# Attention and two MLP layers: row maxima by pair of heads, one turn per pair, and four weight blocks decoded in the first layer

## The chip, the cores and the metric

One core of a Trainium2 chip runs the whole program. The metric is device time in microseconds of one execution; the median of several runs counts. The kernel before was run three times: 1042.83, 1044.88 and 1046.16 us, median 1044.88 us.

## What is computed

The reference, cut to what matters (32 heads of 576 rows and 64 columns, 2304 tokens, widths 512, 2048 and 1024; tau is 0.02):

```python
scores = scale * np.matmul(q, k.transpose(0, 1, 3, 2))
thresh = np.max(scores, axis=-1, keepdims=True) - tau
scores = np.where(scores >= thresh, scores, -1000000000.0)
scores = scores - np.max(scores, axis=-1, keepdims=True)
attn = np.exp(scores)
attn = attn / (np.sum(attn, axis=-1, keepdims=True) + 1e-09)
x = heads_side_by_side(np.matmul(attn, v))

h = x @ w_in                                     # first layer
g = np.where(h >= 1, h, np.where(h <= -1, 0.0, (h + 1) ** 2 / 4))
x = g @ w_out

h = x @ w_in2                                    # second layer
e = np.exp(h - np.max(h, axis=-1, keepdims=True))
solu = h * e / (np.sum(e, axis=-1, keepdims=True) + 1e-09)
ln = (solu - mean(solu)) / np.sqrt(var(solu) + 1e-06) * g_ln
out = ln @ w_out2
```

The four weight matrices arrive as 64-bit floats, which the kernel turns into 32-bit ones itself, block by block ("decoding").

## The kernel before, in words

Engines are named as in the profile: PE multiplies matrices, DVE and ACT work on tiles, POOL too (but not on PSUM, the accumulator memory), and SP issues most transfers. Every fp32 factor is split in a high and a low part, so that three matmuls stand for one product. The order of the instructions on each engine is the order in which the program is written; nothing is reordered afterwards.

**Attention** goes through 16 pairs of heads, nine *units* to a pair, 144 units in all. A unit has 128 key rows of one head; the fifth unit of a pair has the last 64 rows of the first head and the first 64 of the second. For unit u, `attention_unit(u)` runs through a string of letters, each a piece of work:

- S: `scores`, 128 query rows against all 576 keys of a head, four matmuls, and x: `row_max`, the maximum of each row of that tile on DVE. These belong to a later pair, since the maxima of all query rows are wanted before a pair's exponentials. The numbers `S_UNITS` say how many units ahead each of a pair's ten tiles is made.
- A and P, shortly after a head's last tile: `row_shift` (two small operations on ACT, three on POOL) makes the shift from the maxima, `shift_turn` transposes it on PE (tile `tm`), and `shift_store` copies it (tile `mt`) and sends it by a transfer into rows of `q_m`, whence the next product has the shift added.
- E: `shifted`, the shifted scores of the unit, keys by queries (tile `zt`, four matmuls, eight in the shared unit), and `expo` on ACT; M: `mask` on DVE sets to zero what lies below the threshold; p: `p_split` makes high part (`phi`, ACT) and low part (`plo`, POOL) of the unit before; v and V: `values`, the product with V of three units before, six matmuls (`av`).
- P also: `transpose_kq`, five transposes (tile `tr`) for one head of a later pair; F: `split_kq`, high part on ACT and low part `lo` on DVE; T: `stack_k` and `stack_q`, four transfers that put those parts where `scores` and `shifted` read them, and `load_kq` (eight transfers) and `load_v` (three). L: `store_head`.
- J: a step of the decode jobs. A block of 128 x 512 weights is one load, one ACT operation, five DVE operations (L487, L490, L493, L497, L500, on the path `words_to_f32`) and one POOL addition; blocks for use at once then are split on ACT and POOL (`to_sbuf`), others go back to DRAM (`to_dram`). `DECODE` says in which units of a pair which step may run, and `JOB_EVERY` how many units lie between two blocks.

The tiles `sc`, `zt`, `tm` and `tr` share a ring of three PSUM buffers (`ps_r`). A fourth tile must wait until the first has been read: `sc` by `row_max`, `zt` by `mask`, `tm` by the copy to `mt`, `tr` by the split to `lo`.

```python
    ps_r = scores_ps.enter_context(tc.tile_pool(name="ps_r", bufs=3, space=PSUM))
    ...
    jobs = Jobs(parts(("in1", 0), ("out1", 0)) + ahead_out2(0, 1, 2, 3), JOB_EVERY, 2)
```

Twelve blocks are decoded beside the attention: eight of the first layer, and four of the second layer's output weights, ahead of their use.

**First layer.** The 2048 hidden columns are taken in four groups; in each, five chunks of tokens (three of 512, two of 384) meet four blocks of 128 columns. A step n is `moe1_in` (12 matmuls, `h`), `moe1_act` (`cl`, `gh`, `gl` on DVE, ACT and POOL), and `moe1_out` of two steps before (12 matmuls, `y`). Beside a group the blocks of the next are decoded, one begun every three job steps, and what is left at the group's last step is done there at once (`jobs.finish()`). The second layer follows; the change touches nothing in it.

Of the kernel before, what the change touches and what calls it, by code (L numbers as in the profile page):

```python
# [21 lines left out]
def kernel(  # L22
# [45 lines left out]
    ORDER = (  # L68
        "FESvSxvMxxpVPLTASJ",
        "vFEvSSTSxxMxxxpLVPAJ",  # L70
        "EvvvSSSMxxxVLFPATpJ",
        "FESvSSxxMxxpVLPATJ",
        "FESSSMJvxxxpVLPAT",
        "FEvvSSSMxxxpVLPATJ",
        "FvJEvSSSMxxxpVLPAT",
        "FEvvvSSSMxxxVLPvATpJ",
        "FSEvPSSTMxxxpVLAJ",
    )
    STACK = (1, 3)
    V_AT = -5  # L80
    FAST = 2
    V_POOL = 10
    LO_UNITS = ()
    NORM = (13, 5)
    LO_DVE = ()
    T_FIRST = (-17, -17)
    T_SECOND = (-13, -2)
# [4 lines left out]
    DECODE = ('', '', 's', 'asb', '', 's', '', 'as', 'asb')  # L92
# [50 lines left out]
    NBUF = (3, 2)  # L143

    def key_off(h):
        return 64 * (h % 2)

# [29 lines left out]
    def setup_fill(first):  # L177

        for i in range(max(NBUF)):
            for j in range(2):  # L180
# [7 lines left out]
                nc.gpsimd.memset(f32(q_st[j][i][:, S:SP]), 0.0)  # L188
                nc.gpsimd.memset(f32(q_m[j][i][0:D, S:SP]), 0.0)
# [75 lines left out]
    def split_kq(h):  # L265
# [3 lines left out]
        hi = q_st[j][i][:, 0:S]  # L269
# [6 lines left out]
    def stack_k(h):  # L276
        j, i = buf(h)
        kh = f32(q_st[j][i][0:D, 0:S])
        o = slice(key_off(h), key_off(h) + S)
        if h < FAST:  # L280
            nc.scalar.copy(k_on[j][i][0:D, o], kh)
            nc.scalar.copy(q_m[j][i][0:D, 0:S], f32(q_st[j][i][D:P, 0:S]))
# [15 lines left out]
    def scores(h, n):  # L298
        j, i = buf(h)
        o = key_off(h)  # L300
        ps = ps_r.tile([P, 2, 512], F32, tag="r", name="sc")
        for st, kk in ((q_st, k_st), (q_m, k_on)):
            r = slice(0, P if st is q_st else R1)
            for c in range(2):
                nc.tensor.matmul(  # L305
                    ps[:, c, 0:HS],
                    lhsT=st[j][i][r, n * P : n * P + P],
                    rhs=kk[j][i][r, o + c * HS : o + (c + 1) * HS],
                    start=(st is q_st),
                    stop=(st is q_m),  # L310
                )
        sc_ps[h, n] = ps

    def row_max(h, n):
        if n == 0:
            mcol[h] = att_p.tile([P, NTI], F32, tag="mcol", name="mcol", bufs=2)
        mc = mcol[h]
        nc.vector.tensor_reduce(  # L318
            mc[:, n : n + 1], sc_ps.pop((h, n))[:, :, 0:HS], axis=AXES.XY, op=ALU.max, negate=True
        )  # L320

    def row_shift(h):
        mc = mcol.pop(h)


        sh = att_p.tile([P, 2, NTI], F32, tag="sh", name="sh", bufs=2)
        mr = att_p.tile([P, 2, NTI], F32R, tag="mr", name="mr", bufs=2)
        nc.scalar.activation(out=sh[:, 0, :], in_=mc, func=ACTF.Abs, scale=DELTA)
        nc.scalar.activation(out=sh[:, 1, :], in_=sh[:, 0, :], func=ACTF.Relu, bias=ntau[:, 0:1], scale=1.0)
        nc.gpsimd.tensor_tensor(sh[:, 0, :], sh[:, 1, :], mc, op=ALU.add)  # L330
        nc.gpsimd.tensor_copy(mr[:, 0, :], sh[:, 0, :])
        nc.gpsimd.tensor_tensor(mr[:, 1, :], sh[:, 0, :], f32(mr[:, 0, :]), op=ALU.subtract)
        mr_t[h] = mr
# [767 lines left out]
```

## Time and profile before

| what | value |
|---|---|
| three runs, us | 1042.83, 1044.88, 1046.16 |
| the profiled execution's own time, us | 1043.3 |
| its span, first to last instruction, us | 1041.5 |
| PE busy, share of the span | 93% |
| DVE, ACT, POOL busy | 70%, 51%, 57% |
| attention, first to last matmul of the stage | about 6 to 407 us |
| first layer | about 408 to 832 us |
| mean granted clock of PE | 0.993 of full speed |

The time is the execution as the device counts it; the span leaves out 1.8 us around the instructions. A busy share is an average over stages, so the argument goes by stretches. In the rows, L305 is a line of the kernel before, `sc<-k_both,q_st` a matmul that writes tile `sc`, and x4 means four instructions. A time in square brackets behind a row is idle time of that engine before it, and what ended it.

### The profile page before, as it was taken

How to read it: one execution, taken by the hardware profiler on the slowest of the kernel's cores; microseconds unless marked ns; L12 is line 12 of the kernel's file. 1: busy time of each engine (PE TensorE's matmuls, PEld its weight loads, DVE VectorE, ACT ScalarE, POOL GpSimd, SP SyncE). 2: the span in 40 equal slices, each digit the busy share in tenths (PEclk: the TensorE clock that was granted, in tenths of full speed). 3: DMA queues.
4: the chain of work that ended last, by engine and by line, in shares of the span. 5: the costliest groups of instructions: out<-in, count | busy, mean ns of one | idle time of the engine just before them, and what ended most of it. 6: DMA issues, size and time to landing. Idle time of an engine off the chain costs nothing.

```text
span 1041.5 us, 15175 instructions
## 1 busy us (share of the span) xinstructions
PE 969.5 (93%) x5232; PEld 841.7 (81%) x5232; DVE 732.1 (70%) x1133; ACT 535.3 (51%) x1006; POOL 598.0 (57%) x569
## 2 busy tenths in 40 slices
PE   4899899889979998999999999999999999999998
PEld 3788888788878897767887888788888988888886
DVE  3788888868877775588747875787567556666662
ACT  2666666756756666645443443444344534344433
POOL 6577778967786776657524552555256823344332
PEclk9999999989999999999999999999999999999999
DMA  6555556555755520321121112111211104444443
GB/s 155 136 136 135 124 136 160 136 122 131 184 145 126 132 70 24 91 84 59 33 71 61 42 41 81 51 51 41 91 41 51 56 7 132 108 121 127 122 131 91
DMA packets 89885, 99.89 MB, mean 96 GB/s; under 512 B 50032, under 2 KB 62640, under 8 KB 89808
## 3 DMA queue, kind: packets, MB, share of 16 engines
q1 hardware_dynamic: 89424, 98.76, 36.5%
q8 instruction: 41, 0.67, 0.3%
q14 instruction: 36, 0.29, 0.1%
q10 hardware_dynamic: 384, 0.16, 0.1%
HBM read 55.13 MB, written 15.88 MB: 68 GB/s over the span
## 4 chain that ended last, share of the span: by engine, by line
PE 54%; issue 13%; DVE 12%; POOL 10%; ACT 6%; DMA 3%; SPq 2%; ACTq 0%; POOLq 0%; DVEq 0%
PE y L779 10%; PE h L742 10%; PE o L932 10%; PE h L821 9%; PE av L426 6%; PE zt L378 5%; PE sc L305 3%; DVE e L394 3%; POOL gl L763 3%; POOL dec_a L504 2%; POOL plo L403 2%; POOL wg L533 2%; ACT e L389 2%; DVE mcol L318 2%; DMA q_st<-lo 1%
## 5 line engine op out<-in xcount | busy, mean ns | idle before, releaser
L403 POOL TENSOR_TENSOR plo<-e,phi 128x576 fp32r<-128x576 f32 x144 | 206.2, 1438 | 80.7 <-ACT phi L402 79.5
L763 POOL TENSOR_TENSOR gl<-cl,gh 128x512 fp32r<-128x512 f32 (+1 forms) x80 | 96.9, 1211 | 189.4 <-ACT gh L762 156.0
L779 PE MATMUL y<-gh,wg 128*128 128x512 f32 (+1 forms) x640 | 187.6, 374 | 4.1 <-ACT gh L762 4.1
L742 PE MATMUL h<-xh,wg 128*128 128x512 f32 (+1 forms) x640 | 185.8, 371 | 2.0 <-DVE e L394 2.0
L394 DVE SCALAR_TENSOR_TENSOR e<-zt,ntau,e 128x576 f32<-128x576 f32 x144 | 116.6, 810 | 64.9 <-ACT e L389 64.7
L758 ACT ACTIVATE h<-h,mone 128x512 f32<-128x512 f32 (+1 forms) x80 | 49.5, 619 | 198.8 <-DVE cl L757 198.6
L389 ACT ACTIVATE e<-zt 128x576 f32<-128x576 f32 x144 | 93.7, 651 | 96.6 <-PE zt L378 81.1
L779 PEld LDWEIGHTS y<-gh,wg 128*128 128x128 f32 x640 | 117.9, 188 | 24.1 <-ACT gh L762 7.8
L742 PEld LDWEIGHTS h<-xh,wg 128*128 128x128 f32 x640 | 119.0, 189 | 19.2 <-DVE e L394 2.3
L779 PE MATMUL y<-gl,wg 128*128 128x512 f32 (+1 forms) x320 | 122.0, 381 | 10.2 <-POOL gl L763 10.2
L318 DVE TENSOR_REDUCE mcol<-sc 128x1 f32<-128x576 f32 x160 | 116.7, 747 | 10.4 <-PE sc L305 10.4
L757 DVE TENSOR_SCALAR cl<-h 128x512 f32<-128x512 f32 (+1 forms) x80 | 50.8, 635 | 102.0 <-PE h L742 69.0
L742 PE MATMUL h<-xl,wg 128*128 128x512 f32 (+1 forms) x320 | 118.8, 371 | 0.0
L932 PE MATMUL o<-wg,ln 128*128 128x512 f32 x432 | 103.2, 395 | 0.0
L821 PE MATMUL h<-wg,y 128*128 128x512 f32 x432 | 101.2, 390 | 0.0
L402 ACT CAST phi<-e 128x576 fp32r<-128x576 f32 x144 | 96.3, 669 | 2.1 <-DVE e L394 1.9
L932 PEld LDWEIGHTS o<-wg,ln 128*128 128x128 f32 x432 | 81.0, 188 | 19.2
L821 PEld LDWEIGHTS h<-wg,y 128*128 128x128 f32 x432 | 81.0, 188 | 17.0
L896 POOL TENSOR_TENSOR ln<-land,ln 128x1024 fp32r<-128x1024 f32 x16 | 38.5, 2408 | 92.2 <-ACT ln L895 86.4
L378 PE MATMUL zt<-q_st,k_both 128*128 128x288 f32 x320 | 76.9, 322 | 10.4 <-ACT mt L345 5.2
L305 PE MATMUL sc<-k_both,q_st 128*128 128x288 f32 x320 | 73.4, 312 | 13.1 <-DMA q_st<-lo 8.7
L779 PEld LDWEIGHTS y<-gl,wg 128*128 128x128 f32 x320 | 60.1, 188 | 27.3 <-POOL gl L763 19.1
(109 smaller groups left out, 1940.4 us busy)
## 6 DMA issues: line engine op xcount, KB each, us to landing
raw<-in_moe_w_in_dram SPq DMA_DIRECT2D x24, 512.0 KB
raw<-in_moe_w_out_dram SPq DMA_DIRECT2D x24, 512.0 KB
k_both<-q_st SPq DMA_DIRECT2D x30, 288.0 KB
sq<-so SPq DMA_DIRECT2D x64, 128.0 KB
land<-sq SPq DMA_DIRECT2D x16, 512.0 KB
k_both<-lo SPq DMA_DIRECT2D x32, 144.0 KB
q_st<-lo SPq DMA_DIRECT2D x32, 144.0 KB
x<-xs SPq DMA_DIRECT2D x32, 144.0 KB
```

The lines of the kernel that those rows point to most:

```text
L305: nc.tensor.matmul(ps[:, c, 0:HS], lhsT=st[j][i][r, n * P : n * P + P], rhs=kk[j][i][r, o + c * HS : o + (c + 1) * HS], start=(st is q_st) ...
L318: nc.vector.tensor_reduce(mc[:, n : n + 1], sc_ps.pop((h, n))[:, :, 0:HS], axis=AXES.XY, op=ALU.max, negate=True)
L378: nc.tensor.matmul(ps[:, c, 0:HS], lhsT=st, rhs=mv[:, c * HS : (c + 1) * HS], start=(m == 0), stop=(m == len(todo) - 1),)
L389: nc.scalar.activation(out=e, in_=st_ps[u][:, :, 0:HS], func=ACTF.Exp)
L394: nc.vector.scalar_tensor_tensor(out=e, in0=st_ps.pop(u)[:, :, 0:HS], scalar=ntau[:, 0:1], in1=e, op0=ALU.is_ge, op1=ALU.mult)
L402: nc.scalar.copy(hi, e)
L403: (nc.vector if u - NU in LO_DVE or u < NU - UNITS and u % UNITS in LO_UNITS else nc.gpsimd).tensor_tensor(lo, e, f32(hi), op=ALU.subtract)
L742: nc.tensor.matmul(ps, lhsT=a[:, kk, f], rhs=m[:, kk, :], start=(n == 0 and kk == 0), stop=(n == 2 and kk == KD - 1),)
L763: nc.gpsimd.tensor_tensor(gl, cl, f32(gh), op=ALU.subtract)
L779: nc.tensor.matmul(y_ps[c][d], lhsT=a[:, jj, ds_], rhs=m, start=(jj == 0 and n == 0), stop=(jj == JG - 1 and n == 2),)
L821: nc.tensor.matmul(ps[g], lhsT=a[:, kk, :], rhs=wg_t["in2", g][s][:, kk, :], start=(n < 2), stop=(n >= 6 * KD - 2),)
L932: nc.tensor.matmul(ps, lhsT=a[:, f, :], rhs=wg_t["out2", f // 4][m][:, f % 4, :], start=(n == 0), stop=(n == len(terms) - 1))
```

## The change

Row maxima are made by pair. A pair's 1152 query rows now stand in nine tiles of 128, where each head had five for itself, the fifth half empty: the last 64 query rows of the first head and the first 64 of the second share tile 4, into which eight matmuls accumulate. To that end the queries of the second head lie 64 columns further on (`on(h)`), with zeros in the pad, as the keys did already. One `row_max` is left out per pair, and the shared column of maxima is copied on POOL. From the second pair on there is one `row_shift` and one turn for both heads; the store is still two transfers.

All units have the same string of letters, with one tile of scores at its start. Tiles are made 14 to 6 units ahead (10 to 2 before), transposes of keys and queries 22 and 16 units ahead (16 and 10). To hold more heads at a time the second head has three buffers instead of two; `e` has 3 instead of 4 buffers, `phi` and `plo` 4 instead of 5, `xs` and `mt` 1 instead of 2.

Only eight blocks are decoded beside the attention, one begun every 14 units; the four blocks of the second layer's output weights go to the first layer's groups, one more each in the first two and two more in the third.

```diff
-    T_A, T_B = -16, -10
-    S_UNITS = (-10, -9, -7, -7, -6, -5, -4, -3, -3, -2)
+    T_A, T_B = -22, -16
+    S_FIRST = -14
...
-    JOB_EVERY = 9
-    ORDER = (
-        "FESvSxvMxxpVPLTASJ",
...
-    )
+    JOB_EVERY = 14
+    ORDER = "SxFEvMvpVLPATJ"
...
-    V_AT = -5
+    V_AT = -2
-    T_SECOND = (-13, -2)
+    T_SECOND = (-13, -7)
-    DECODE = ('', '', 's', 'asb', '', 's', '', 'as', 'asb')
+    DECODE = ('asb', 's', 'asb', 'a', 'sb', 'asb', 'a', 's', 'asb')
-    NBUF = (3, 2)
+    NBUF = (3, 3)
...
-    def scores(h, n):
+    S_ORDER = (0, 1, 2, 3, 5, 4, 6, 7, 8)
+    def scores(p, n):
         ps = ps_r.tile([P, 2, 512], F32, tag="r", name="sc")
+        todo = []
+        for h in ([2 * p] if n <= 4 else []) + ([2 * p + 1] if n >= 4 else []):
+            j, i = buf(h)
+            at_ = slice((n - 4 * j) * P, (n - 4 * j) * P + P)
+            for st, kk, r in ((q_st, k_st, P), (q_m, k_on, R1)):
+                todo.append((st[j][i][0:r, at_], kk[j][i][0:r, on(h)]))
...
-    def row_max(h, n):
+    def row_max(p, n):
...
+        m = n + (n > 4)
         nc.vector.tensor_reduce(
...
+        if n == 4:
+            nc.gpsimd.tensor_copy(mc[:, 5:6], mc[:, 4:5])
...
-        for j in range(2):
-            t = UNITS * p + S_UNITS[NTI * j + NTI - 1]
-            at(act_, t + 1, row_shift, 2 * p + j)
...
+        for js, last in ((slice(0, 1), 4), (slice(1, 2), 8)) if p == 0 else ((slice(0, 2), 8),):
+            t = UNITS * p + S_FIRST + S_ORDER.index(last)
+            at(act_, t + 1, row_shift, p, js)
+            at(pe_, t + TURN_AT, shift_turn, p, js)
+            at(act_, t + TURN_AT, shift_store, p, js)
...
-    jobs = Jobs(parts(("in1", 0), ("out1", 0)) + ahead_out2(0, 1, 2, 3), JOB_EVERY, 2)
+    jobs = Jobs(parts(("in1", 0), ("out1", 0)), JOB_EVERY, 2)
...
-        parts(("in1", 1), ("out1", 1)) + ahead_out2(4, 5),
-        parts(("in1", 2), ("out1", 2)) + ahead_out2(6, 7),
-        parts(("in1", 3), ("out1", 3)) + ahead_in2(*IN2_AHEAD),
+        parts(("in1", 1), ("out1", 1)) + ahead_out2(0, 1, 2),
+        parts(("in1", 2), ("out1", 2)) + ahead_out2(3, 4, 5),
+        parts(("in1", 3), ("out1", 3)) + ahead_out2(6, 7) + ahead_in2(*IN2_AHEAD),
```

The order of the instructions at three places, before and after. The numbers behind `k_both`, `q_st` and `q_m` tell buffers of different heads apart.

PE at a turn, in the middle of the attention. Before:

```order
L305 MATMUL sc<-k_both_102,q_st_107 128x288 x2
L305 MATMUL sc<-k_both_102,q_m_112 128x288 x2
L426 MATMUL av<-plo,v_hi_117 128x288 x2
L339 MATMUL tm<-ident,mr 10x128
L378 MATMUL zt<-q_st_108,k_both_103 128x288 x2
L378 MATMUL zt<-q_m_113,k_both_103 128x288 x2
```

After:

```order
L382 MATMUL zt<-q_m_114,k_both_102 128x288 x2
L430 MATMUL av<-phi,v_hi_119 128x288 x2
L430 MATMUL av<-phi,v_lo_121 64x288 x2
L430 MATMUL av<-plo,v_hi_119 128x288 x2
L341 MATMUL tm<-ident,mr 20x128
L301 MATMUL sc<-k_both_101,q_st_107 128x288 x2
L301 MATMUL sc<-k_both_101,q_m_113 128x288 x2
L382 MATMUL zt<-q_st_108,k_both_102 128x288 x2
```

The next `zt` stood right behind the turn; now the turn stands at a unit's end, and a tile of scores comes between it and the next `zt`.

DVE at the very start (`lo` rows are the splits of heads 0, 1, 2, 3 and so on). Before:

```order
L271 SCALAR_TENSOR_TENSOR lo<-tr,scale_120,q_st_104 128x576
L271 SCALAR_TENSOR_TENSOR lo<-tr,scale_120,q_st_107 128x576
L271 SCALAR_TENSOR_TENSOR lo<-tr,scale_120,q_st_105 128x576
L318 TENSOR_REDUCE mcol<-sc 128x1 x10
L271 SCALAR_TENSOR_TENSOR lo<-tr,scale_120,q_st_108 128x576
L318 TENSOR_REDUCE mcol<-sc 128x1 x2
L394 SCALAR_TENSOR_TENSOR e<-zt,ntau,e 128x576 x3
```

After:

```order
L262 SCALAR_TENSOR_TENSOR lo<-tr,scale_123,q_st_105 128x576
L262 SCALAR_TENSOR_TENSOR lo<-tr,scale_123,q_st_108 128x576
L315 TENSOR_REDUCE mcol<-sc 128x1 x3
L262 SCALAR_TENSOR_TENSOR lo<-tr,scale_123,q_st_106 128x576
L315 TENSOR_REDUCE mcol<-sc 128x1 x6
L262 SCALAR_TENSOR_TENSOR lo<-tr,scale_123,q_st_109 128x576
L315 TENSOR_REDUCE mcol<-sc 128x1 x3
L262 SCALAR_TENSOR_TENSOR lo<-tr,scale_123,q_st_107 128x576
L315 TENSOR_REDUCE mcol<-sc 128x1 x3
L398 SCALAR_TENSOR_TENSOR e<-zt,ntau,e 128x576
```

The split of head 2 stood ahead of all row maxima and now stands behind three; 15 maxima instead of 12 and one more split stand ahead of the first mask.

DVE at the last step of the first layer's second group. Before:

```order
L757 TENSOR_SCALAR cl<-h_7033 128x384
L761 TENSOR_TENSOR cl<-cl,h_6989 128x384
L497 TENSOR_SCALAR raw<-dec_a 128x512
L500 SCALAR_TENSOR_TENSOR raw<-raw 128x512
L757 TENSOR_SCALAR cl<-h_7075 128x512
L761 TENSOR_TENSOR cl<-cl,h_7033 128x384
```

After:

```order
L766 TENSOR_TENSOR cl<-cl,h_6769 128x384
L501 TENSOR_SCALAR raw<-dec_a 128x512
L504 SCALAR_TENSOR_TENSOR raw<-raw 128x512
L491 TENSOR_SCALAR dec_a<-dec_a 128x512
L494 TENSOR_SCALAR dec_a<-dec_a 128x512
L497 SCALAR_TENSOR_TENSOR dec_a<-raw,dec_a 128x512
L501 TENSOR_SCALAR raw<-dec_a 128x512
L504 SCALAR_TENSOR_TENSOR raw<-raw 128x512
L762 TENSOR_SCALAR cl<-h_6866 128x512
L766 TENSOR_TENSOR cl<-cl,h_6813 128x384
```

All five DVE operations of the added block stand behind the group's last step and ahead of the next step's `cl`. It is so at the end of the first group too, and at the end of the third with two blocks, ten operations.

## Rows read from the trace of the kernel before

**Rows 1.** Windows of one pair each, with decoding and without: busy us (count) by engine.

```profile
57.90:82.00 24.10, 21.90 (x154) 20.08 (x153) 20.87 (x27) 16.31 (x31) 18.62 (x18) 1.00 0.57 133
343.30:365.60 22.30, 21.07 (x153) 19.88 (x152) 16.50 (x23) 15.20 (x29) 15.84 (x17) 1.00 0.50 115
```

**Rows 2.** Waits of PE, 28 to 407 us: us in total, times, longest.

```profile
PE tr L262 <- DVE e L394: 8.6, 14, 1.0
PE tm L339 <- DVE e L394: 6.3, 12, 0.8
PE zt L378 <- ACT mt L345: 5.2, 15, 0.3
PE sc L305 <- DMA q_st<-lo: 5.1, 3, 4.1
PE zt L378 <- DVE lo L271: 4.1, 8, 0.6
```

**Rows 3.** Chain of waits, 0 to 460 us: start, us, what.

```profile
15.47 2.73 DMA q_st<-lo
...
343.26 1.07 PE sc L305 x8
```

**Rows 4.** Timeline of PE: start, us, line, operation.

```profile
13.35 1.38 PE L262 MATMUL tr<-ident,nat 128*128 128x128 f32 x5 [3.90 <-DMA nat<-in_k_dram]
...
28.51 0.42 PE L378 MATMUL zt<-q_st,k_both 128*128 128x288 f32 x2
...
192.59 0.80 PE L262 MATMUL tr<-ident,nat 128*128 128x128 f32 x5
...
197.88 0.27 PE L339 MATMUL tm<-ident,mr 128*10 128x128 f32 x1
...
209.87 0.82 PE L305 MATMUL sc<-k_both,q_st 128*128 128x288 f32 x2 [4.13 <-DMA q_st<-lo]
...
386.04 0.54 PE L378 MATMUL zt<-q_st,k_both 128*128 128x288 f32 x2 [0.34 <-ACT mt L345]
...
402.61 0.42 PE L378 MATMUL zt<-q_st,k_both 128*128 128x288 f32 x2
```

**Rows 5.** Window after PE's longest wait: PE, PEld, DVE, ACT, POOL busy, clock, DMA.

```profile
209.90:214.90 5.00, 5.00 (x21) 4.93 (x22) 1.31 (x2) 1.24 (x3) 1.20 (x4) 0.50 0.76 165
```

**Rows 6.** Timelines of DVE and SP at the start of the program.

```profile
18.32 0.82 DVE L271 SCALAR_TENSOR_TENSOR lo<-tr,scale,q_st 128x576 fp32r<-128x576 f32 x1 [7.24 <-DMA q_st<-lo]
...
21.59 0.76 DVE L318 TENSOR_REDUCE mcol<-sc 128x1 f32<-128x576 f32 x1 [0.20 <-PE sc L305]
...
32.51 0.46 SPq L293 DMA_DIRECT2D q_st<-lo  x1
```

**Rows 7.** Timeline of DVE in a pair with decoding.

```profile
180.06 0.81 DVE L271 SCALAR_TENSOR_TENSOR lo<-tr,scale,q_st 128x576 fp32r<-128x576 f32 x1
180.78 0.74 DVE L318 TENSOR_REDUCE mcol<-sc 128x1 f32<-128x576 f32 x1
181.45 0.80 DVE L394 SCALAR_TENSOR_TENSOR e<-zt,ntau,e 128x576 f32<-128x576 f32 x1
182.18 0.95 DVE L500 SCALAR_TENSOR_TENSOR raw<-raw 128x512 f32<-128x512 uint32 x1
```

**Rows 8.** Groups of DVE instructions, 57.9 to 106.1 us: busy us, mean ns.

```profile
L490 DVE TENSOR_SCALAR dec_a<-dec_a 128x512 uint32<-128x512 uint32 x2 | 3.3, 1631 | 0.0
```

**Rows 9.** First layer, around group ends: timelines of DVE and PE.

```profile
615.52 0.67 DVE L487 TENSOR_SCALAR dec_a<-dec_a 128x512 f32<-128x512 f32 x1
...
618.84 0.69 DVE L500 SCALAR_TENSOR_TENSOR raw<-raw 128x512 f32<-128x512 uint32 x1
...
731.87 0.69 DVE L500 SCALAR_TENSOR_TENSOR raw<-raw 128x512 f32<-128x512 uint32 x1
733.67 0.69 DVE L757 TENSOR_SCALAR cl<-h 128x512 f32<-128x512 f32 x1 [1.11 <-POOL gl L763]
...
738.33 0.52 PE L779 MATMUL y<-gh,wg 128*128 128x384 f32 x2
```

More of the change, by code (lines that the diff above doesn't have):

```diff
@@ L306, in scores @@
                     ps[:, c, 0:HS],
[L307 to L310, printed above, removed]
-                )
-        sc_ps[h, n] = ps
-    def row_max(h, n):
-        if n == 0:
-            mcol[h] = att_p.tile([P, NTI], F32, tag="mcol", name="mcol", bufs=2)
-        mc = mcol[h]
+                    lhsT=st,
+                    rhs=mv[:, c * HS : (c + 1) * HS],
@@ L318, in row_max @@
+                    start=(m == 0),
+                    stop=(m == len(todo) - 1),
+                )
+        sc_ps[p, n] = ps
+    def row_max(p, n):
+        if p not in mcol:
+            mcol[p] = att_p.tile([P, 2, NTI], F32, tag="mcol", name="mcol", bufs=2)
+        mc = mcol[p].rearrange("p j n -> p (j n)")
+        m = n + (n > 4)
         nc.vector.tensor_reduce(
-            mc[:, n : n + 1], sc_ps.pop((h, n))[:, :, 0:HS], axis=AXES.XY, op=ALU.max, negate=True
+            mc[:, m : m + 1], sc_ps.pop((p, n))[:, :, 0:HS], axis=AXES.XY, op=ALU.max, negate=True
@@ L320, in row_max @@
         )
[L322 to L333, printed above, removed]
@@ new lines, with row_shift @@
+    mr_t = {}
+    def row_shift(p, js):
+        mc = mcol[p][:, js, :]
+        sh = att_p.tile([P, 2, 2, NTI], F32, tag="sh", name="sh", bufs=2)
+        mr = att_p.tile([P, 2, 2, NTI], F32R, tag="mr", name="mr", bufs=2)
+        s0, s1, m0, m1 = sh[:, 0, js], sh[:, 1, js], mr[:, js, 0, :], mr[:, js, 1, :]
+        nc.scalar.activation(out=s0, in_=mc, func=ACTF.Abs, scale=DELTA)
+        nc.scalar.activation(out=s1, in_=s0, func=ACTF.Relu, bias=ntau[:, 0:1], scale=1.0)
+        nc.gpsimd.tensor_tensor(s0, s1, mc, op=ALU.add)
+        nc.gpsimd.tensor_copy(m0, s0)
+        nc.gpsimd.tensor_tensor(m1, s0, f32(m0), op=ALU.subtract)
+        mr_t[p, js.start] = mr[:, js]
@@ new lines, in shift_turn, with shift_store @@
+    def shift_turn(p, js):
+        ps = ps_r.tile([P, 1024], F32, tag="r", name="tm")
+        mr = f32(mr_t.pop((p, js.start))).rearrange("p j l n -> p (j l n)")
+        nc.tensor.transpose(ps[0 : mr.shape[1], 0:P], mr, ident)
+        mr_t[p, js.start] = ps[0 : mr.shape[1], 0:P]
+    def shift_store(p, js):
+        mt = att_p.tile([4 * NTI, P], F32R, tag="mt", name="mt", bufs=1)
+        ps = mr_t.pop((p, js.start))
+        nc.scalar.copy(mt[0 : ps.shape[0]], ps)
+        for n, h in enumerate(range(2 * p + js.start, 2 * p + js.stop)):
+            j, i = buf(h)
+            nc.scalar.dma_start(f32(q_m[j][i][R1:R3, :]), f32(mt[2 * NTI * n : 2 * NTI * n + 2 * NTI, :]))
@@ L387, in expo @@
     def expo(u):
-        e = att_p.tile([P, 2, HS], F32, tag="e", name="e", bufs=4)
+        e = att_p.tile([P, 2, HS], F32, tag="e", name="e", bufs=3)
         nc.scalar.activation(out=e, in_=st_ps[u][:, :, 0:HS], func=ACTF.Exp)
@@ L399, in p_split @@
         e = e_t.pop(u)
-        hi = att_p.tile([P, 2, HS], F32R, tag="phi", name="phi", bufs=5)
-        lo = att_p.tile([P, 2, HS], F32R, tag="plo", name="plo", bufs=5)
+        hi = att_p.tile([P, 2, HS], F32R, tag="phi", name="phi", bufs=4)
+        lo = att_p.tile([P, 2, HS], F32R, tag="plo", name="plo", bufs=4)
         nc.scalar.copy(hi, e)
-        (nc.vector if u - NU in LO_DVE or u < NU - UNITS and u % UNITS in LO_UNITS else nc.gpsimd).tensor_tensor(lo, e, f32(hi), op=ALU.subtract)
+        nc.gpsimd.tensor_tensor(lo, e, f32(hi), op=ALU.subtract)
         ph_t[u] = (hi, lo)
@@ L434, in store_head @@
         if h < NH - 2:
-            xs = att_p.tile([P, 2, HS], F32, tag="xs", name="xs", bufs=2)
+            xs = att_p.tile([P, 2, HS], F32, tag="xs", name="xs", bufs=1)
         else:
@@ L691, in attention_unit @@
         mx = iter(s_at.get(u, ()))
-        for what in ORDER[u % UNITS]:
+        for what in ORDER:
             if what == "E" and 0 <= u < NU:
```

52 lines of the change are left out of this document (15 added, 37 removed).

## The prediction, made before the changed kernel ran

> **What bounds the kernel now.** I read the page by engine first: PE is busy for 93% of the span, so only what lets PE work without gaps, or takes work from it, can pay. The change lies in the attention and in the first layer, so next come windows of one pair of heads. A pair with a decoded block lasts 24.1 us, one without 22.3 us; PE issues some 153 matmuls in both, and DVE is busy for 20.87 and 16.50 us of them [rows 1]. So a block costs 1.8 us of the attention, and DVE does not set the pace alone: PE waits between bursts. The table of PE's waits says for what. Three of the five are waits for a ring buffer (`tr` and `tm` for the mask of an earlier `zt`, `zt` for the copy `mt`), 20.1 us in all; `zt` waits 4.1 us for `lo`, and three late transfers cost 5.1 us [rows 2]. The chain and the timeline give PE's floor: eight matmuls of 288 columns in a row take 1.07 us, five transposes at most 0.80, a turn at most 0.27 [rows 3, 4]. A pair has 140 such matmuls, two sets of transposes and, after the change, one turn: 140 x 1.07 / 8 + 1.60 + 0.27 = 20.6 us, or 2.29 us a unit. Both kinds of pair lie above that, by 1.7 and 3.5 us. That is what there is to win here.
>
> The sum is made against the profiled execution, 1043.3 us (span 1041.5 and 1.8 around it); it is 1.6 us below the median of 1044.88.
>
> **The units that hold scores.** Before, the last tile of scores is made in unit 133, and from the first `zt` (28.51) to that unit's (386.04) are 357.5 us, 2.69 a unit. After the change the last tile is in unit 129, so 130 units hold scores.
> - Floor: 130 x 2.29 = 297.5 us. The matmuls of the tile left out are not saved, since the shared tile takes eight; a turn less per pair is in the floor already.
> - Eight blocks remain, at the 1.8 us that a block costs now [rows 1]: 14.4 us. Bounds: nothing, if DVE's room hides them, and 4.4 us each, the whole difference in DVE's busy time. I take the measured price, though the neighbours change: the maximum left out takes off 0.74 us of DVE per pair, while the changed order puts most blocks' five steps into five units in a row.
> - Ring waits: the buffer that `tm` or `tr` takes over was that of the unit before, whose mask is long done; behind `tm` comes a tile of scores, so `zt` meets `mt` late; the wait for `lo` passes to the second tile of scores behind `tr`. A DVE on time needs 0.67 us for the maximum and 0.72 for the split (start to start, [rows 7]); PE comes for that buffer 2.29 - 0.53 = 1.76 us after the scores. That is just in time, so I leave 0.3 us a pair, 4.3 us for 14.4 pairs; bounds are 0 and the 1.7 us of today's pair without a block, 24 us.
>
> Sum: 316 us for 130 units, 2.43 each.
>
> **The start.** The split of head 2 began at 18.32 [rows 6]. Now it stands behind three row maxima. The third begins at 21.59 [rows 6], later by head 2's transposes, which now lie between tiles of scores (1.38 us, [rows 4]), and takes 0.76: the split begins at 23.7, 5.4 us later. On SP behind it stand the stacking of head 2, eleven loads and the stacking of head 3, the same transfers as before, loads of keys and queries now ahead of those of values; all in order, so the last transfer of head 3 goes from 32.51 [rows 6] to 37.8. It lands 2.73 later [rows 3], at 40.6. Before, no early `zt` hung on it; now two tiles of pair 1 that read head 3 (12 matmuls, 1.6 us) stand ahead of the first `zt`. So that comes at 42.1 instead of 28.51. PE is nearly idle for some microseconds before. After its longest wait of today, 4.13 us, it ran the next 5 us at a granted clock of 0.50, which is 1.2 GHz [rows 4, 5], and lost 2.5 us; I add the same. Bounds for both: 6 and 18 us.
>
> **The tail.** Without scores a unit takes (402.61 - 386.04) / 10 = 1.66 us [rows 4]. From the `zt` of unit 130 to that of 143 are 13 x 1.66 = 21.5 us, where it was ten units. The change moves nothing in these units but the size of three buffers.
>
> The last `zt`: 42.1 + 2.5 + 316.2 + 21.5 = 382.3, against 402.61 [rows 4]: **20.3 us earlier**.
>
> **Smaller buffers, DMAs, other queues.** `e`, `phi` and `plo` lose a buffer each; the unit's values run three units behind, so four `plo` still do. SP loses the four blocks' loads and stores, about 8 issues; ACT issues as many stores of `mt` as before, two at a time once a pair. Heads are stacked three to five units ahead of their first tile (two to three before), which covers the late transfers of [rows 2]. POOL gets one tiny copy per pair. I count all this at nothing; what hides it is POOL's idle 5.5 us in a pair [rows 1], and one queue late by a unit would cost about 2.4 us each time.
>
> **The first layer.** A block on DVE takes 618.84 + 0.69 - 615.52 = 4.0 us [rows 9]. By the order the added ones stand behind a group's last step, ahead of the next `cl`. At the third end DVE was done with decoding at 731.87 + 0.69 = 732.6 [rows 9]. With two more blocks `cl` starts at 740.6 instead of 733.67; it takes 0.69, and the addition and the two parts that follow, as three steps of its kind, about 2 us more: 743.3. PE wants that at 738.33 and waits 5 us. With one block `cl` starts at 736.6 and PE waits 0 to 1: 1 us each at the first two ends. Sum **7 us**; bounds 0 (all covered by PE's four `h` buffers) and 16 (four blocks in full).
>
> The decode step L490 takes 1.63 us in the attention [rows 8], where POOL is busy for 77% of a pair [rows 1]. The Trainium skill, "SBUF — State Buffer", section "SBUF: two separate sides", says that DVE and GpSimd (POOL) share a pair of ports under an exclusive lock, and that whoever comes second is fully blocked until the other's instruction ends. By that rule a block would be cheaper at a group's end, where POOL waits for `gh`, and the 7 us would be nearer 5; the row of 4.0 us is from such a stretch already, so my sum keeps it.
>
> **Sum:** 1043.3 - 20.3 + 7 = **1030.0 us**.
>
> **The rivals.**
> 1. *Decoding is hidden.* One maximum less and fewer blocks leave DVE room, so the eight blocks cost PE nothing. For it: DVE is at 87% in today's worst pairs [rows 1] and gets 0.74 us less. Against: five steps in successive units. Time: 1030 - 14.4 = 1016.
> 2. *Slower: a decode step delays the next unit's maximum and split in full.* The place is DVE's queue: a step of up to 1.63 us [rows 8] follows the mask, and behind it stand the maximum and the split on whose buffers PE's next tiles wait, with no unit of respite between two steps. If a block's 4.4 us reach PE whole, the price is 8 x 2.6 = 21 us more: 1051. It decides from 1.8 + 13.3 / 8 = 3.5 us a block. Against: the ring now gives the maximum a whole unit.
> 3. *The change does not do what it says.* Ring waits only change places, and a pair without a block stays at 22.3 us: 14.4 x 1.4 = 20 us more, 1050. For it: the ring still has three buffers for the same operations, and with smaller `e` and `plo` POOL may come late. Against: the 20.1 us of [rows 2] hang on an order that is gone.
>
> **How the numbers follow.** My forecast has a chance of 0.55, with a range of its own from 1018 to 1041 by its bounds (the start 7 us shorter, the first layer 5 us either way, ring waits from 0 to 0.9 us a pair). Rival 1 has 0.20, rival 2 has 0.12, rival 3 has 0.13. A measurement of this kernel tells about 0.3%, 3.1 us, from no change; so faster means below 1041.7 and slower above 1048. Forecast and rival 1 lie below but for a little of the forecast: 0.72. Rivals 2 and 3 in part strength end near no change: 0.12; in full they are slower: 0.16. The range of 8 in 10 reaches to rival 1's better half and to the milder halves of 2 and 3: 1012 to 1048.
>
> **What would show it.** First `zt` near 42 us and the last near 382; a pair near 20.9 us without and 22.7 with a block; the waits of `tr` and `tm` for masks gone from PE's list, and `zt` no longer waiting for `mt`; a granted clock of half for some microseconds after 40 us; at the end of the first layer's third group a wait of about 5 us of `y` for `gh`. The prediction is wrong if a pair without a block stays above 22 us, if a block costs over 3.5 us, or if a new wait (`e` for POOL, `xs` for its store) stands high in the lists of ACT or PE.

## The result, and the profile after

The changed kernel is slower by 1.2%: 1057.26 us, median of four runs (1056.14 to 1058.10), against 1043.86 for the kernel before in the same comparison; ratio 1.0122, 95% interval 1.0104 to 1.0139. The forecast was 1030.0, its range 1012 to 1048. The profiled execution took 1056.5 us (span 1054.7). Against the forecast's own terms:

| term | before | forecast | after |
|---|---|---|---|
| first `zt`, us | 28.51 | 42.1 | 43.24 |
| first to last `zt` | 374.1 | 340.2 | 356.5 |
| last `zt` | 402.61 | 382.3 | 399.72 |
| first layer, first `h` to the second layer's first `h` | 423.6 | 430.6 | 439.0 |
| profiled execution | 1043.3 | 1030.0 | 1056.5 |

So the start came as forecast. The units between missed by 16 us, and the first layer by 8. PE's waits in the attention, 28 to 407 us, after the change (us in total, times, longest):

```profile
PE zt L382 <- DVE mcol L315: 8.4, 10, 1.1
PE sc L301 <- DVE mcol L315: 8.3, 14, 0.8
PE av L430 <- ACT xs L442: 7.5, 10, 1.5
PE sc L301 <- DMA q_st<-lo: 4.8, 1, 4.8
PE sc L301 <- DVE lo L262: 2.2, 6, 0.4
```

The waits of [rows 2] for masks and for `mt` are gone but for 0.2 us, as the prediction said. In their place stand 16.7 us for row maxima (`mcol`), and 7.5 us of the values `av` for the copy `xs`. ACT's list for the same stretch puts 12.6 us of `e` down to `plo` (11 times), which was the other new wait that the prediction named as a sign against it. That line must not be taken at its word: eight of the eleven, 11.5 us together, stand right behind two stores of `mt` that ACT issues itself, as at this turn:

```profile
82.55 0.25 ACT L347 CAST mt<-tm 20x128 fp32r<-20x128 f32 x1
82.83 1.31 ACTq L350 DMA_DIRECT2D q_m<-mt  x2
84.24 0.65 ACT L393 ACTIVATE e<-zt 128x576 f32<-128x576 f32 x1 [1.44 <-POOL plo L407]
```

The issue of both stores ends at 84.14, a tenth of a microsecond before `e` begins. In the kernel before, a turn sent one store, and its issue took 0.62 us.

The start on PE's timeline, and the last `zt`, which answer to [rows 4]:

```profile
40.22 0.82 PE L301 MATMUL sc<-k_both,q_st 128*128 128x288 f32 x2 [4.81 <-DMA q_st<-lo]
...
43.24 0.68 PE L382 MATMUL zt<-q_st,k_both 128*128 128x288 f32 x2
...
399.72 0.42 PE L382 MATMUL zt<-q_st,k_both 128*128 128x288 f32 x2
```

The tile of pair 1 that reads head 3 waits for that head's transfer. The matmuls after it run at half rate (the window 43.24 to 46 has a granted clock of 0.50, or 1.2 GHz).

Windows of two pairs of the attention, which answer to [rows 1], and of two stretches behind the ends of the first layer's second and third group (length; busy us and count of PE, PEld, DVE, ACT, POOL; clock; DMA share and GB/s):

```profile
152.39:177.60 25.21, 22.07 (x154) 20.03 (x151) 21.00 (x28) 15.51 (x29) 16.61 (x15) 1.00 0.56 131
177.60:199.16 21.56, 21.17 (x151) 19.93 (x152) 15.29 (x21) 15.06 (x28) 19.09 (x18) 1.00 0.60 148
...
630.00:640.00 10.00, 7.92 (x30) 6.49 (x29) 5.07 (x9) 3.50 (x6) 3.58 (x3) 0.83 0.57 184
740.00:750.00 10.00, 2.79 (x10) 1.75 (x9) 4.61 (x10) 2.47 (x5) 3.57 (x3) 0.66 0.37 111
```

A pair without a decode step lasts 21.6 us (22.3 before), one with all five steps of a block 25.2 (24.1 before). From one turn to the next, over the twelve pairs from the turn at 58.69 to that at 339.69, a pair takes 23.42 us; the prediction had 22.05 (its floor and waits of 20.9, and eight blocks of 1.8 us over the 12.5 pairs that they last when one is begun every 14 units). At the third group's end PE is idle for most of ten microseconds. SP, ACT, DVE and PE there, one timeline each:

```profile
732.47 0.38 SPq L519 DMA_DIRECT2D raw<-in_moe_w_in_dram  x1
737.40 0.33 SPq L542 DMA_DIRECT2D w_out_f<-dec_a  x1
737.82 0.93 SPq L519 DMA_DIRECT2D raw<-in_moe_w_in_dram  x1
```

```profile
736.53 0.68 ACT L489 ACTIVATE dec_a<-raw 128x512 f32<-128x512 f32 x1 [1.51 <-DMA raw<-in_moe_w_in_dram]
742.23 0.66 ACT L489 ACTIVATE dec_a<-raw 128x512 f32<-128x512 f32 x1 [5.02 <-DMA raw<-in_moe_w_in_dram]
```

```profile
742.92 0.43 DVE L491 TENSOR_SCALAR dec_a<-dec_a 128x512 f32<-128x512 f32 x1 [2.87 <-ACT dec_a L489]
...
745.03 0.69 DVE L504 SCALAR_TENSOR_TENSOR raw<-raw 128x512 f32<-128x512 uint32 x1
745.64 0.68 DVE L762 TENSOR_SCALAR cl<-h 128x512 f32<-128x512 f32 x1
```

```profile
748.10 1.01 PE L784 MATMUL y<-gh,wg 128*128 128x384 f32 x2 [7.14 <-ACT gh L767]
```

Read from the bottom: `y` waits 7.14 us for `gh`; `gh` comes from `cl`, which stands on DVE behind a block's five steps; those wait for ACT, ACT for the raw weights, and that load is issued on SP behind the store of the block before. The five steps themselves take only 2.8 us (742.92 to 745.72), against the 4.0 of [rows 9]. It is the load that is late.

### The profile page after: what moved, and what is told of

It reads as the page before. It is cut to its first block, busy times and chain, and to the rows that moved or that the text cites. A ratio compares the mean times of both kernels' runs of the same rounds, so it can differ in the third digit from the quotient of the medians.

```text
span 1054.7 us, 14974 instructions
## 1 busy us (share of the span) xinstructions
PE 971.6 (92%) x5217; PEld 843.2 (80%) x5217; DVE 728.0 (69%) x1117; ACT 523.4 (50%) x961; POOL 591.7 (56%) x547
## 5 line engine op out<-in xcount | busy, mean ns | idle before, releaser
L407 POOL TENSOR_TENSOR plo<-e,phi 128x576 fp32r<-128x576 f32 x144 | 209.0, 1454 | 87.1 <-ACT phi L406 76.2
L784 PE MATMUL y<-gh,wg 128*128 128x512 f32 (+1 forms) x640 | 190.3, 379 | 14.7 <-ACT gh L767 14.7
L315 DVE TENSOR_REDUCE mcol<-sc 128x1 f32<-128x576 f32 x144 | 107.8, 749 | 37.4 <-PE sc L301 37.3
L301 PE MATMUL sc<-k_both,q_st 128*128 128x288 f32 x320 | 77.8, 326 | 26.0 <-DMA q_st<-lo 13.6
L301 PEld LDWEIGHTS sc<-k_both,q_st 128*128 128x128 f32 x320 | 53.3, 200 | 34.6 <-issue 14.4
```

The source lines that it names most:

```text
L301: nc.tensor.matmul(ps[:, c, 0:HS], lhsT=st, rhs=mv[:, c * HS : (c + 1) * HS], start=(m == 0), stop=(m == len(todo) - 1),)
L315: nc.vector.tensor_reduce(mc[:, m : m + 1], sc_ps.pop((p, n))[:, :, 0:HS], axis=AXES.XY, op=ALU.max, negate=True)
L407: nc.gpsimd.tensor_tensor(lo, e, f32(hi), op=ALU.subtract)
L784: nc.tensor.matmul(y_ps[c][d], lhsT=a[:, jj, ds_], rhs=m, start=(jj == 0 and n == 0), stop=(jj == JG - 1 and n == 2),)
```

## The experiments

All fifteen leave the computation whole. Times are medians; ratios are against the kernel before on the same chip, whose medians lie between 1043.25 and 1045.28 us. "A pair" is the mean over twelve pairs from turn to turn (`tm`), from the third turn in PE's timeline on.

| run | us | ratio, 95% | a pair | first layer |
|---|---|---|---|---|
| changed kernel | 1057.26 | 1.0104 to 1.0139 | 23.42 | 439.0 |
| layer_only | 1046.16 | 0.9988 to 1.0032 | | 438.7 |
| att_only | 1050.71 | 1.0034 to 1.0071 | 24.3 | 421.9 |
| no_blocks | 1087.02 | 1.0367 to 1.0432 | 21.74 | 439.0 |
| no_blocks_xs | 1072.83 | 1.0253 to 1.0298 | 21.03 | 439.3 |
| spread | 1045.28 | 0.9999 to 1.0034 | 22.44 | 438.6 |
| rotated | 1051.39 | 1.0040 to 1.0092 | 22.91 | 437.4 |
| xs_first | 1045.22 | 1.0000 to 1.0035 | 22.61 | 439.3 |
| every2 | 1045.12 | 0.9996 to 1.0042 | 23.4 | 426.5 |
| start2 | 1053.12 | 1.0055 to 1.0110 | 23.4 | 439.1 |
| start3 | 1055.62 | 1.0092 to 1.0160 | 23.3 | 438.8 |
| three | 1030.88 | 0.9835 to 0.9881 | 22.31 | 429.1 |
| four | 1022.96 | 0.9776 to 0.9805 | 22.31 | 426.6 |
| twelve | 1028.37 | 0.9824 to 0.9860 | 23.1 | 422.0 |
| four_twelve | 1024.65 | 0.9793 to 0.9838 | 23.1 | 421.9 |
| layer_every2 | 1033.26 | 0.9874 to 0.9941 | | 429.4 |

The two runs without blocks decode all eight at one place late in the attention, so their total times say nothing; they are there for the length of a pair. In the three runs with twelve blocks, "a pair" is one with a block. The last `zt` below is the last row of it in the timeline (399.98 in the changed kernel, 402.88 before).

### The two halves of the change

layer_only is the kernel before with the blocks moved; att_only the changed kernel with them moved back:

```diff
# layer_only, on the kernel before (att_only: the reverse, on the changed kernel)
-    jobs = Jobs(parts(("in1", 0), ("out1", 0)) + ahead_out2(0, 1, 2, 3), JOB_EVERY, 2)
+    jobs = Jobs(parts(("in1", 0), ("out1", 0)), JOB_EVERY, 2)
-        parts(("in1", 1), ("out1", 1)) + ahead_out2(4, 5),
+        parts(("in1", 1), ("out1", 1)) + ahead_out2(0, 1, 2),
...
-    JOB_EVERY = 9
+    JOB_EVERY = 14
```

> The kernel before with only the decoding moved: eight blocks beside the attention, one begun every 14 units, and the plan of the changed kernel in the first layer. Theory (the moved blocks cost the first layer 15 us by themselves, through late loads at the ends of the groups): first layer near 439 us instead of 424, attention 4 x 1.8 = 7 us shorter, time about 1052 us. Rival (the first layer is slower only because of the state in which the changed attention leaves it): first layer near 424, time about 1037.

> The changed kernel with its attention, but with the four blocks back beside the attention, one begun every 9 units, and the first layer's plan as before. Theory (4 us a block in the new attention): last zt some 16 us later than in the changed kernel, at about 416 us, first layer back from 439 to 424 us, so the time hardly moves: about 1057 us. If a block costs 1.8 us: last zt 407, time about 1049. If blocks are hidden: last zt 400, time 1042.

layer_only: the first layer takes 438.7 us, as in the changed kernel, and the first `h` comes 10.6 us earlier (397.97 against 408.58). The total is unchanged. So the layer's 15 us belong to the move of blocks, whatever the attention does. The rival falls. My 1052 was too high, since the old attention got 10.6 us shorter, not 7. (The same attention in layer_every2 below has its first `h` at 392.95, some 5 us sooner; most of the difference is there by the third pair's turn.) The timelines show why. In the kernel before, a pair (from one first turn to the next) with all five steps of a block lasts 24.1 us as a rule, one with none 22.0 to 22.4. In layer_only, where a block is begun every 14 units, pairs with blocks hold two to four steps, and most of them last 22.4 to 22.8. So the 1.8 us of [rows 1] was the price of a whole block in one pair; spaced further, blocks cost the old attention little.

att_only: last zt 409.5 (four blocks more cost 9.5 us), layer 421.9, and 1050.71 us, below the 1057 that 4 us a block would have given and nearest to the case of 1.8. Where each pair holds exactly one block, it lasts 24.30 us:

```profile
107.31:131.61 24.30, 22.08 (x151) 20.11 (x152) 21.29 (x26) 15.32 (x29) 18.14 (x16) 1.00 0.63 132
```

### What a pair is without blocks

```diff
-    JOBS_FROM = -1
+    JOBS_FROM = 1000
...
         attention_unit(u)
+        if u == NU - 13:
+            jobs.finish()
```

no_blocks_xs has besides the edit of xs_first, shown below.

> The changed kernel with no block decoded before unit 131; all eight are then decoded at one place, in the units that hold no scores. Nothing of the computation is left out. The mean pitch of a pair from 60 to 340 us was 23.42 us with the blocks. Theory (a block's five steps on DVE reach PE nearly in full, about 4 us each, 8 blocks in 14.4 pairs): pitch near 21.2 us. If a block costs the 1.8 us of the prediction: 22.4. Rival (the smaller buffers of e, plo and xs hold the pairs up, whatever is decoded): 23.0 or more.

> The run without blocks before unit 131, with xs ahead of phi where a head ends; nothing of the computation is left out. Theory (without blocks only the waits for xs keep a pair above its floor): most pairs last 20.8 to 21.1 us instead of 21.5, and only pairs beside the reciprocals last longer. Rival (the floor of 20.6 was too low, and something else in PE's own work fills a pair): 21.3 us or more.

Most pairs without blocks last 21.5 us, so a block in each of att_only's pairs costs 24.3 - 21.5 = 2.8 us. In the changed kernel DVE's groups count 38 decode steps, or 7.6 blocks, in that stretch: 12 x (23.42 - 21.74) / 7.6 = 2.7 us a block. The expected 4 was too high, the predicted 1.8 too low. Of what remains without blocks, the list of PE's waits (59 to 320 us) names `xs` first:

```profile
PE av L430 <- ACT xs L442: 5.3, 11, 0.7
PE zt L382 <- DVE mcol L315: 1.6, 2, 0.8
```

With `xs` ahead of `phi` these are gone, and a pair lasts 20.9 us:

```profile
99.64:120.56 20.92, 20.78 (x154) 19.89 (x151) 14.97 (x21) 14.57 (x27) 14.94 (x14) 1.00 0.55 124
```

That is the length that the prediction gave a pair without a block, 20.6 of floor and 0.3 of ring waits. The rival falls. The 0.3 is not ring waits, though: PE's list of this run (59 to 320 us) has none, and PE is busy for 20.78 of the 20.92 us.

### The wait for xs

```diff
-        for what in ORDER:
+        for what in "SxFEvMvVLpPATJ" if u % UNITS in (2, 7) else ORDER:
```

> The changed kernel with the values and the copy xs of a finished head ahead of phi in the two units of a pair that finish a head. Theory (without blocks a pair stays 0.9 us above its floor of 20.6, and 0.5 of that is the next head's values waiting for xs): the waits of av for xs fall from 7.5 us to under 2, a pair gets 0.4 us shorter, last zt 5 us earlier, time about 1052 us. Rival (xs waits for the values themselves, and phi comes late instead): last zt within 2 us of 399.7 or later.

The mean pair went from 23.42 to 22.61 us, the last `zt` to 389.0, PE's waits for `xs` from 7.5 us to 1.8, the time to 1045.22: twice what was expected. The other half of the gain stands in the list too: the waits for `mcol` went from 16.7 us to 10.3 with them. How `xs` comes late, one head's end in no_blocks shows; ACT, POOL and PE:

```profile
102.00 0.66 ACT L406 CAST phi<-e 128x576 fp32r<-128x576 f32 x1
102.56 0.25 ACT L347 CAST mt<-tm 20x128 fp32r<-20x128 f32 x1
102.84 1.27 ACTq L350 DMA_DIRECT2D q_m<-mt  x2
104.22 0.65 ACT L393 ACTIVATE e<-zt 128x576 f32<-128x576 f32 x1 [1.41 <-POOL plo L407]
104.77 0.66 ACT L406 CAST phi<-e 128x576 fp32r<-128x576 f32 x1
105.33 0.64 ACT L442 COPY xs<-av 128x576 f32<-128x576 f32 x1
```

```profile
100.28 1.43 POOL L407 TENSOR_TENSOR plo<-e,phi 128x576 fp32r<-128x576 f32 x1
102.74 1.43 POOL L407 TENSOR_TENSOR plo<-e,phi 128x576 fp32r<-128x576 f32 x1 [1.03 <-ACT phi L406]
```

```profile
103.30 0.43 PE L382 MATMUL zt<-q_m,k_both 67*128 67x288 f32 x2
...
106.03 0.53 PE L430 MATMUL av<-phi,v_hi 128*128 128x288 f32 x2 [0.45 <-ACT xs L442]
```

The change put the copy `xs` behind `phi`, and `phi` stands behind `e`. All this time the one PSUM tile of `av` is held, and the next head's values stand first in PE's queue. `e` itself is late, and the list names POOL's `plo`, but the rows say otherwise. With three buffers `e` takes over the one of three units before, whose `plo` ended at 101.71 (100.28 + 1.43); the `plo` that the list names began at 102.74, behind the `phi` of 102.00, and is of only two units before. `zt` was done at 103.73 (103.30 + 0.43). What ends just before `e` is the issue of the two stores of `mt`, at 104.11. Since one turn serves both heads, both stores stand in the unit ahead of the same head's end. All eleven waits for `xs` of the list above lie 4.0 to 4.4 us behind a turn, that is at the first head's end of a pair; at the second head's end, where `xs` stands behind `phi` too but no store ahead, there is none. One store of 0.62 us would have ended at about 103.5, before `zt`, by estimate. So two things have to come together, the order of `xs` and `phi` and the two stores. The first is shown by the runs with `xs` ahead; the second is read from the timelines, and no run moves a store.

### The price of a block

spread takes the table of the kernel before; rotated the same table two units earlier:

```diff
-    DECODE = ('asb', 's', 'asb', 'a', 'sb', 'asb', 'a', 's', 'asb')
+    DECODE = ('', '', 's', 'asb', '', 's', '', 'as', 'asb')   # spread
+    DECODE = ('s', 'asb', '', 's', '', 'as', 'asb', '', '')   # rotated
```

> The changed kernel with the table of the kernel before for the units in which a decode step may run (five of nine, fewer next to each other), all eight blocks still beside the attention. Theory (a block costs 2.8 to 2.9 us because its steps stand in successive units and leave DVE no unit to catch up): 1.7 to 2.0 us a block, last zt 7 to 9 us earlier than 399.7, time about 1049 us. Rival (each step costs the same wherever it stands, since PE's next tile waits for the maximum behind it): last zt within 2 us of 399.7, time about 1057.

> The changed kernel with the decode steps as far apart as in the run with the old table, but each two units earlier in the pair, so that two of them now share a unit with a split of keys and queries. Theory (the distance between steps sets a block's price): last zt within 3 us of that run's 388.1. Rival (it is which units they share, those with a split being the costly ones): last zt between 393 and 400.

spread: last `zt` 388.1, 1045.28 us. A block costs 12 x (22.44 - 21.74) / 7.8 = 1.1 us instead of 2.7 (39 steps stand in that stretch here), though its steps are hardly shorter (the five mean durations add to 6.4 us in the changed kernel, 5.8 here). What differs is the distance. The waits for `mcol` go from 16.7 us to 4.3:

```profile
PE av L430 <- ACT xs L442: 9.8, 14, 1.5
PE sc L301 <- DMA q_st<-lo: 4.8, 1, 4.8
PE zt L382 <- DVE mcol L315: 2.4, 4, 1.0
PE sc L301 <- DVE mcol L315: 1.9, 6, 0.3
```

rotated: last `zt` 395.2, a block 1.8 us (40 steps, or 8 blocks). My expectation fell: with the same distances, but more steps in units with a split of keys and queries, about half of the gain is lost. So both count. By the order of DVE's rows, none of the changed kernel's 40 steps stands in a unit with a split, 9 of spread's and 20 of rotated's; a unit with a step follows another directly 22, 13 and 12 times. The changed kernel's table keeps clear of the units with a split, yet fills all the others.

How a step can be so long on DVE, two steps of the changed kernel show, and POOL beside them:

```profile
124.44 1.58 DVE L491 TENSOR_SCALAR dec_a<-dec_a 128x512 f32<-128x512 f32 x1
125.94 0.74 DVE L315 TENSOR_REDUCE mcol<-sc 128x1 f32<-128x576 f32 x1
...
127.34 0.97 DVE L494 TENSOR_SCALAR dec_a<-dec_a 128x512 uint32<-128x512 uint32 x1
```

```profile
124.30 1.43 POOL L407 TENSOR_TENSOR plo<-e,phi 128x576 fp32r<-128x576 f32 x1 [0.97 <-ACT phi L406]
...
126.59 1.43 POOL L407 TENSOR_TENSOR plo<-e,phi 128x576 fp32r<-128x576 f32 x1
```

L491 took 0.43 us at 742.92, with POOL idle. Here it takes 1.58, and ends 0.3 us behind the `plo` that began before it (124.30 + 1.43 = 125.73; 126.02). L494 ends 0.3 us behind the next one (128.02; 128.31). The maximum, which reads PSUM, takes 0.75 beside POOL (at 122.15, beside the `plo` of 121.91) and 0.74 without. The rule that the prediction cited from the Trainium skill, "SBUF — State Buffer", section "SBUF: two separate sides", is that DVE, in an operation in a 2-port mode or with two SBUF inputs, and GpSimd take a shared pair of ports for a whole instruction, and that the other is blocked meanwhile. The trace agrees, with those two ends; in which mode L491 and L494 ran, no row shows.

### The blocks in the first layer

```diff
-    EVERY = (3, 3, 3, 2, 2, 2)
+    EVERY = (2, 2, 2, 2, 2, 2)
```

> The changed kernel with the blocks of the first layer's first three groups begun every two job steps instead of three. Theory (the added blocks cost what they cost because they are begun last and wait for their loads at a group's end): the waits of 1.5 and 5.0 us for the raw loads leave ACT's list, y no longer waits 7 us for gh, first layer 422 to 428 us instead of 439, time about 1045 us. Rival (a block costs the layer 3.8 us through its own work on DVE, ACT and POOL, wherever it stands): first layer stays at 437 or more, time about 1057.

First layer 426.5 us, time 1045.12. On ACT's list from 690 to 760 us no wait for a raw load is left, and PE's list for the layer (405 to 845 us) has no long wait any more:

```profile
PE y L784 <- POOL gl L768: 10.9, 18, 0.9
PE y L784 <- ACT gh L767: 6.9, 8, 1.7
```

In the changed kernel the second line reads 14.7 us, 12 times, longest 7.1. So four blocks cost 426.5 - 421.9 (att_only) = 4.6 us when they are begun in time, 1.2 each, and 17 when not. The rival falls.

### The start

start2 transposes heads 2 and 3 earlier; start3 makes the five tiles that read head 3 later:

```diff
-    T_SECOND = (-13, -7)
+    T_SECOND = (-15, -12)     # start2
...
             t = UNITS * p + S_FIRST + k_
+            if p == 1 and k_ > 3:     # start3
+                t = (3, 3, 4, 5, 5)[k_ - 4]
```

> The changed kernel with the transposes of heads 2 and 3 three and five units earlier (at units -15 and -12), so that their stacking goes out ahead of the loads of the next pair. Theory (the start is held by the last transfer of head 3): first zt at about 36 us instead of 43.2, the wait of 4.8 us gone, time 7 us less, about 1050 us. Rival (PE's clock and the number of tiles ahead of the first zt set the start, not the transfer): first zt within 2 us of 43.2.

> The changed kernel with the five tiles of scores of pair 1 that read head 3 made in units 3 to 5 instead of units -1 to 3, so that the first zt stands ahead of them, and the turn of pair 1 at unit 7. Theory (only head 3's transfer and the half clock after the wait hold the start): first zt at about 36 us, no wait of 4.8 us for that transfer, last zt 6 to 8 us earlier than 399.7, time about 1050 us. Rival (the work left out ahead of the first zt comes back whole behind it, on DVE or PE): last zt within 2 us of 399.7.

Neither did what I expected. In start2 the wait of 4.8 us is gone, but the first `zt` came at 40.89 and the last one 3.5 us earlier, since PE ran its tiles slowly for longer: 0.68 us a pair of matmuls until about 40 us, with no long wait before. In start3 the first `zt` came at 38.28, and the last one at 401.0: what was left out ahead came back behind. At that `zt`, PE's rows were still the slow ones:

```profile
38.28 0.68 PE L382 MATMUL zt<-q_st,k_both 128*128 128x288 f32 x2
```

In the changed kernel a pair of these matmuls takes 0.43 us from about 30 us on, until the wait at 35; in start2, from 18.32 on, there was no wait over 0.9 us. The moment differs from run to run of the same order of work: in every2, where nothing of the start was changed, the rows are slow throughout and the first `zt` is at 44.64 instead of 43.24.

### All together

> The changed kernel with three edits that each took some 11 us by itself: blocks of the first layer's first groups begun every two job steps, the old table for the decode steps, xs ahead of phi where a head ends. Theory (three separate losses, in different places): they add, last zt 377 to 381, first layer 426 to 428, time 1022 to 1028 us. Rival (the two in the attention take away the same wait twice): last zt 386 to 389, time 1033 or more.

> The run with three edits, and the transposes of heads 2 and 3 three and five units earlier as in the run on the start. Theory (the start is a separate loss too): 3.5 us less than with three edits, about 1019 to 1025 us. Rival (the shorter start comes back later): within 1 us of the run with three edits.

> The changed kernel with the old table for the decode steps, xs ahead of phi, and the four blocks of the second layer back beside the attention, one begun every 9 units; the first layer's plan and pace as in the kernel before. So the maxima by pair without the move of blocks. Theory (a spaced block costs 1.2 us in the attention and about 1.2 us in the first layer when it is begun in time): last zt 4 to 6 us later than with three edits, first layer 422, time within 2 us of the run with three edits. If the move itself is worth something: 3 us or more behind it.

> The kernel before with its own attention, eight blocks beside it (one begun every 14 units), the changed kernel's plan in the first layer, and that layer's blocks begun every two job steps. So the move of four blocks, with their loads in time, without the maxima by pair. Theory (the move is worth what the attention saves, 10.6 us to the first h, less 3 to 5 us in the layer): first h at 398, first layer 427 to 429, time 1036 to 1040 us. Rival (blocks in the layer cost as much as they save): within 3 us of the kernel before.

> The run with four edits, but with the four blocks of the second layer beside the attention, one begun every 9 units, and the first layer's plan and pace as in the kernel before. Theory (a spaced block costs 0.8 to 1.2 us in the attention and 1.2 us in the layer if begun in time, so the place does not matter): within 3 us of the 1022.96 of the run with four edits. Rival (the move is worth 7 us, as a block's price of 1.8 us would have it): 1028 us or more.

three (every2, spread, xs_first) gave 1030.88 us, last `zt` 388.1. The losses do not add: a pair takes 22.31 us, against 22.44 and 22.61 with one edit of the attention. A spaced block, worth 1.1 us where `xs` is late, costs 12 x (22.31 - 21.03) / 7.8 = 2.0 once it is not. That DVE catches up while PE waits for `xs` would explain it; it is not shown, and another part is new: with `phi` behind `xs`, PE's list in three begins with 3.2 us of `av` for `plo` (7 times). So the rival was right of the attention, though the time came out between the two. four (three and start2) gave 1022.96, 7.9 us less, more than the 3.5 expected: start2's edit helps, and three's own start was a slow one (third turn at 61.19, 54.67 in four), so not all of it is the edit's. four is the best: 2.1% below the kernel before, interval 2.0 to 2.2%.

twelve and four_twelve put the four blocks back beside the attention: 1028.37 and 1024.65, 2.5 below and 1.7 above the runs beside them. So the place of these blocks hardly matters once they are spaced in the one and begun in time in the other. In the old attention the move with loads in time is worth something: layer_every2 takes 1033.26 (ratio 0.9908), somewhat better than expected, which fits the little that spaced blocks cost there. From there to four are 10 us. That is about what the maxima by pair bring with order, table and start mended; the two ran on different chips.

## Why the prediction was wrong, step by step

- **The start** (first `zt` 42.1): right, 43.24, by the transfer of head 3 and at half clock, as written. Its steps came true as well: the split of head 2 began at 23.68 (23.7 said), the last transfer of head 3 was issued at 37.81 (37.8 said; 32.51 + 5.4 is 37.9), and PE went on at 40.22 (40.6 said). The experiments add that two other orders of the start gave back 3.5 us and nothing.
- **The floor** (20.6 us a pair, 0.3 for ring waits): right in size. 20.9 us in no_blocks_xs; the twelve-pair mean is 21.03, as pairs beside the reciprocals last up to 21.6. The 0.3 was luck, as no ring wait is left in that run.
- **"Smaller buffers, DMAs, other queues. I count all this at nothing"**: this step failed, at "ACT issues as many stores of `mt` as before, two at a time once a pair". The two together hold ACT for 1.3 us just ahead of a head's end, so `e` starts late; `phi` stands behind `e`, and with one order of letters for all units `xs` stands behind `phi`. The late `xs` is worth 0.7 us a pair without blocks (21.74 - 21.03), 10 us over 14.4 pairs. The prediction priced "one queue late" and then did not follow ACT's queue at a head's end. It looked for danger in POOL and the smaller buffers; the rows of a head's end show no wait for either.
- **Eight blocks at 1.8 us each**: mis-sized. They cost 2.7, some 7 us more. The prediction saw the cause ("the changed order puts most blocks' five steps into five units in a row") and kept the old price, which was itself that of five steps in one pair and fell when layer_only spaced them. spread shows that cause at work. Rival 2 had the mechanism; its deciding price of 3.5 us wasn't reached.
- **The ring waits change places** (rival 3, 22.3 us without a block): no. 21.6 us in the changed kernel, 20.9 without the wait for `xs`.
- The three misses explain the last `zt`: 10 + 7 + 1.1 of the start, with 1.9 for the pairs beside the reciprocals, less some 2.4 us because the first three units hold no values (18 matmuls of 0.134 us, which the floor counts): 17.6 us, and 399.72 - 382.3 = 17.4. So close a sum is in part luck. Read directly, the units with scores missed by 14.8 us (first `zt` to that of unit 130 at 376.71, 333.5 us, against 316.2 + 2.5), and the tail by 1.5 (23.0 against 21.5), with 2.0 us of waits for `xs` in it.
- **The first layer, 7 us**: mechanism half right, size wrong. The place was right (the group ends, above all the third, with `y` waiting for `gh`), and waits of 1, 1 and 5 us became 1.84, 1.61 and 7.14, 10.6 in all. But the prediction took DVE's steps for the cause, which take 2.8 us there and not 4.0. It also took the 4.0 of [rows 9] for a stretch with POOL out of the way; POOL was at work there (from 615.86, 1.48 us), and L490 took 1.40 us and ended 0.28 behind it. The loads on SP, which it counted as issues removed from the attention, are late in the layer. And it left out that the clock falls again after these waits: 0.83 in 630 to 640 us, 0.61 in 748 to 755, which is 0.17 x 10 + 0.39 x 7 = 4.4 us, by estimate. 10.6 + 4.4 is nearly the whole 15.4. But the kernel before had lost some 1.6 us of its own at the layer's start (clock 0.69 in 410 to 415 us), so 17 us are to be explained, as against att_only, and about 2 stay open.

## What to carry to other kernels

When a table of orders is replaced by one order for all units, follow each engine's queue once through the rare units (a head's end, a store), not only through the common one, and count the time in which it issues transfers. Where a list names what a wait ended with, ask whether that was needed at all: here it named POOL, and the engine was issuing its own stores. The price of a piece of filler work is that of its place: the same five steps cost PE 1.1 to 2.8 us a block in the new attention, by how far apart they stand and which units they share. A block of work added at a stage's end needs its load issued early, so count the queue that loads, not only the engine that computes; and losses that meet in the same units need not add up when they are mended.

## What the runs showed that was not expected

- A wait of only 1.61 us of PE (at 633.03) was followed by ten microseconds at a mean granted clock of 0.83, while one of 1.84 us (at 524.90) was followed by none below 1.00.
- Between about 18 and 50 us, when PE's matmul rows pass from 0.68 to 0.43 us a pair differs by many microseconds between runs of the same order of work. In three they are still slow at 46 to 52 us, where the granted clock of the window reads 1.00; why the two disagree stays open.
- Beside POOL's `plo`, DVE's decode steps between SBUF tiles grow from 0.43 to 1.58 us, while operations on PSUM keep their 0.74 to 0.82.
